# Phase carry through DRAM and GpSimd, phases kept in the arctangents' buffer, slot sums taken by the exponential

## The chip, the cores and the metric

The kernel runs on one core of one Trainium2 chip. The metric is the device time of one execution in microseconds (us). Three runs of the kernel before are shown, and one further execution was profiled; all durations, waits and gaps below come from that profiled execution.

## The reference

All is fp32. A gated linear attention (4 batches, 8 heads, 768 steps, head width 48) feeds a mixture of experts in which every expert owns 4 slots, and that feeds a two-layer network with a leaky ReLU:

```
scale = minimum(mag, 0.999) / (mag + 1e-06)          # mag = |a|
a_re_n, a_im_n = a_re * scale, a_im * scale
for t in range(768):
    new_re = ar * S_re - ai * S_im                   # the complex decay of step t
    new_im = ar * S_im + ai * S_re
    S_re, S_im = new_re + k[t] (x) v[t], new_im
    y[t] = q[t] . S_re
x = y as 3072 x 384
logits = x @ phi                                     # 32 slots
slot_input = softmax over tokens(logits).T @ x       # 32 x 384
slot_out[e] = relu(slot_input[e] @ w1[e]) @ w2[e]    # 8 experts, F = 1024
x = softmax over slots(logits) @ slot_out
out = leaky(x @ w_in) @ w_out                        # 384 -> 2048 -> 384
```

## The kernel before

**Units.** The attention is cut into 12 units: 6 chunks of 128 steps times 2 pairs of batches. Steps lie on the partitions, and a row of 768 columns holds 16 groups (2 batches x 8 heads) of width 48. Unit u and unit u+2 are the same sequences, one chunk later. The recurrence is done in chunks: with the logarithm of the decay's modulus and its phase summed over the steps of a chunk, q and k are multiplied by exp, cos and sin (`prep4`, L623 and L632), and attention in the chunk is a masked product (`mB` to `mC`, L662, L665, L688), to which the state `S` of the earlier chunks is added; `mD` (L703, L713 to L716) brings the state forward by the decay column `dc`.

**The phase of a unit.** `prep2` (L554) takes the arctangent in place in the buffer `im` on ScalarE. From the third unit on, GpSimd then starts a DMA that adds the carried phase to row 0 of `im` (L557). `phase` multiplies by a triangle of 1/2pi on TensorE (L570, `tri_p`), so that each row is the running sum in turns. ScalarE adds a large constant to round it (L581), VectorE subtracts it and the sum again (L582), which leaves minus the part of a turn in `cs[:, 1]`, and a bitwise AND puts its magnitude into `cs[:, 0]` (L583). `prep3` takes the two sines in place (L593, L594). For the unit two further on, VectorE multiplies rows 96 to 127 of `cs[:, 1]` by -2pi into a buffer `cr` of the tag `w` (L586), of which only row 127 is used.

**The decay of a unit.** `decay` (L606, L607) takes two exponentials of the running sum; its last row goes by SyncE's queue to a DRAM buffer `dr` and comes back as the columns `dc` (L611, L613). The same queue carries all loads, in order.

**Slots.** After each second unit `slots` forms the logits of 512 steps (L748), their running maximum, the exponential `e` with the maximum as bias (L756), and the products for `acc`; VectorE sums `e` along its rows (L778, in the first round L782) and updates the denominator `den` (L779).

**After the attention.** The expert weights come in 64 slabs of 384 KB into buffers as they become free (`load_slabs`; tag `w` has 33 buffers). `layer1` (L924) and `layer2` (L960) use them, then `product` and the two layers of the network (L1022, L1039 to L1041) follow.

**What sets the order.** The program is written as operations with costs, and a planner (`Plan.emit`, `backward`, `forward`) orders every engine's instructions by them: it repeats a backward and a forward pass and keeps the order with the earliest planned end. A different cost or a different operation can therefore move instructions on all engines. The table functions of ScalarE keep a fixed order among themselves (`turns`). Buffers are handed out by tags with a fixed number of buffers; a load waits on SyncE's queue until its buffer is free, and what is queued behind it waits too.

Of the kernel before, what the change touches and what calls it, by code (L numbers as in the profile page):

```python
# [24 lines left out]
P = 128  # L25
# [3 lines left out]
W = G * D  # L29
# [67 lines left out]
class Plan:  # L97
# [9 lines left out]
    def add(self, eng, cost, fn, r=(), w=(), table=None, nbytes=0, after=()):  # L107
        o = Op()
        if eng == "SP":
            cost = 0.06 + nbytes / 0.36e6  # L110
# [209 lines left out]
def tile_kernel(  # L320
# [69 lines left out]
    t_dr = Tag(dram, "dr", [W], 3)  # L390
# [93 lines left out]
    def cuts(u):  # L484
        return parts.get(u, [(0, W)])
# [64 lines left out]
    def prep2(u):  # L550

        im = st[u]["im"]
        for o, e in cuts(u):
            table(("A", u), "T", e - o, lambda x=slice(o, e): A.activation(im()[:, x], im()[:, x], AF.Arctan), [], [(im, o)])  # L554
        if u >= 2:
            cr = st[u - 2]["cr"]
            plan.add("POOL", 1.0, lambda: GP.dma_start(im()[0:1, :], cr()[127:128, :], accum_op=ALU.add), [cr], [(im, o) for o, _ in cuts(u)], nbytes=3072)  # L557
# [14 lines left out]
    def phase(u):  # L572
# [5 lines left out]
        for (ct, c0), (o, e) in zip(piles(u, (b_tr, b_tr, b_c)), cu):  # L578
            n, x, z = e - o, slice(o, e), slice(o - c0, e - c0)
            pe(n / 600 + 0.02, lambda ct=ct, c0=c0, o=o, e=e: sums(ct, c0, [(tri_p, im)], o, e), [(im, o)], [(ct, o)])  # L580
            act(n + 100, lambda x=x, z=z, ct=ct: A.activation(cs()[:, 1, x], ct()[:, z], AF.Identity, bias=b_rnd), [(ct, o)], [(cs, 1, o)])  # L581
            dve(c_dve(n), lambda x=x, z=z, ct=ct: V.scalar_tensor_tensor(cs()[:, 1, x], cs()[:, 1, x], RND, ct()[:, z], op0=ALU.subtract, op1=ALU.subtract), [(ct, o)], [(cs, 1, o)])  # L582
            dve(c_dve2(n), lambda x=x: V.tensor_scalar(cs()[:, 0, x].bitcast(I32), cs()[:, 1, x].bitcast(I32), 0x7FFFFFFF, None, op0=ALU.bitwise_and), [(cs, 1, o)], [(cs, 0, o)])  # L583
        if u + 2 < NU:
            cr = s["cr"] = t_w()
            dve(c_dve2(W), lambda: V.tensor_scalar(cr()[96:128], cs()[96:128, 1], -TWO_PI, None, op0=ALU.mult), [(cs, 1, o) for o, _ in cu], [cr])  # L586

    def prep3(u):

        cs = st[u]["cs"]  # L590
        for o, e in cuts(u):
            n, x = e - o, slice(o, e)
            table(("S", u), "T", n, lambda x=x: A.activation(cs()[:, 1, x], cs()[:, 1, x], AF.Sin, scale=-TWO_PI), [], [(cs, 1, o)])  # L593
# [144 lines left out]
    def slots(c):  # L738
# [17 lines left out]
        table(("L", c), "E", 128, lambda: A.activation(e(), b()[:, :P], AF.Exp, bias=n1), [b, ("nm", c + 1)], [e])  # L756
# [17 lines left out]
        sm = t_sm()  # L774
        sm1 = lambda: sm()[:, 0:1]
        if c:
            dve(c_dve(384), lambda: V.scalar_tensor_tensor(acc, acc, al(), b3()[:, :DM], op0=ALU.mult, op1=ALU.add), [b3, al], ["acc"])
            dve(0.2, lambda: V.tensor_reduce(sm1(), e(), axis=AX.X, op=ALU.add), [e], [sm])  # L778
            dve(0.1, lambda: V.scalar_tensor_tensor(den, den, al(), sm1(), op0=ALU.mult, op1=ALU.add), [sm, al], ["den"])  # L779
        else:  # L780
            dve(c_dve(384), lambda: V.tensor_copy(acc, b3()[:, :DM]), [b3], ["acc"])
            dve(0.2, lambda: V.tensor_reduce(den, e(), axis=AX.X, op=ALU.add), [e], ["den"])  # L782
# [361 lines left out]
```

## Time and profile before

| what | us |
|---|---|
| three runs, median (lowest to highest) | 513.94 (513.3 to 515.96) |
| the profiled execution, whole | 515.49 |
| its span in the trace | 513.6 |
| PE, DVE, ACT busy in the span | 480.4, 330.5, 357.5 |
| share of the last-ending chain: PE, DVE, ACT, DMA | 66%, 19%, 7%, 4% |

PE is TensorE's matrix products, DVE VectorE, ACT ScalarE, POOL GpSimd, SP SyncE. The span is 1.9 us shorter than the execution. Three stages are to be told apart by their windows: the attention from about 20 to 250 us, the experts from 252 to 284 us, and the two-layer network from 284 us to the end. The busy time of PE is modelled for pipelined matrix products, so where it reads full it has to be compared with how closely the products follow each other.

### The profile page before, as it was taken

To read this page: it belongs to the slowest core of one execution; us is meant where nothing else is said; L and a number is where in the kernel's file an instruction comes from. 1 tells how busy PE (TensorE), PEld (TensorE's weight loads), DVE (VectorE), ACT (ScalarE), POOL (GpSimd) and SP (SyncE) were. 2 spreads that over 40 slices of the span, in tenths; PEclk is the share of its full clock that TensorE was granted. 3 is DMA by queue.
4 is the path that set the end of the run, shared out by engine and by line. 5 is a ranking of instruction groups with operands and counts; after the bars stand their busy time and mean duration, and the time that the engine had idled before them with its cause. 6 is when DMAs were issued, how large, how long until landed. Compare 5 with 4: busy or idle time off the path is not lost.

```text
span 513.6 us, 10264 instructions
## 1 busy us (share of the span) xinstructions
PE 480.4 (94%) x3985; PEld 433.8 (84%) x3985; DVE 330.5 (64%) x705; ACT 357.5 (70%) x702; POOL 13.0 (3%) x27
## 2 busy tenths in 40 slices
PE   2597989999999999999799999999999999999997
PEld 1386868888889888889554899999999999999997
DVE  3597999999999998997533999514500552025300
ACT  6799999999989999864203899339900993069502
POOL 1000000000000000001000000000000000000000
PEclk9999999999999999999899999999999999999999
DMA  7955254364543757579799321000000110010102
GB/s 254 392 164 158 60 186 154 95 170 141 155 125 126 238 165 247 176 252 368 251 367 387 111 61 33 1 32 30 33 1 0 47 47 2 1 46 2 46 1 92
DMA packets 43844, 66.97 MB, mean 130 GB/s; under 512 B 19098, under 2 KB 24970, under 8 KB 43796
## 3 DMA queue, kind: packets, MB, share of 16 engines
q1 hardware_dynamic: 43476, 66.29, 38.9%
q8 instruction: 31, 0.51, 0.4%
q0 software_dynamic: 320, 0.03, 0.1%
q14 instruction: 17, 0.14, 0.1%
HBM read 61.53 MB, written 4.75 MB: 129 GB/s over the span
## 4 chain that ended last, share of the span: by engine, by line
PE 66%; DVE 19%; ACT 7%; DMA 4%; issue 2%; SPq 1%; POOL 0%; ACTq 0%; DVEq 0%; POOLq 0%
PE b L1039 13%; PE b L1040 13%; PE b L1041 13%; PE b L1022 4%; PE bsc L662 4%; PE bm L688 4%; PE btr L647 3%; PE b L924 2%; DVE sc L665 2%; PE bc L570 2%; DVE k L632 2%; PE bsc L703 2%; PE b L960 2%; DVE q L632 2%; DVE w L526 2%
## 5 line engine op out<-in xcount | busy, mean ns | idle before, releaser
L1026 DVE TENSOR_TENSOR w<-x,w 128x384 fp32r<-128x384 f32 x128 | 67.8, 554 | 106.0 <-ACT w L1025 105.9
L1039 PE MATMUL b<-w 128*128 128x384 f32 x384 | 128.6, 335 | 0.8 <-ACT x L1024 0.8
L1040 PE MATMUL b<-w 128*128 128x384 f32 x384 | 128.7, 335 | 0.0
L1041 PE MATMUL b<-w 128*128 128x384 f32 x384 | 128.3, 334 | 0.0
L1039 PEld LDWEIGHTS b<-w 128*128 128x128 f32 x384 | 72.1, 188 | 1.0 <-ACT x L1024 1.0
L1041 PEld LDWEIGHTS b<-w 128*128 128x128 f32 x384 | 72.1, 188 | 0.0
L1040 PEld LDWEIGHTS b<-w 128*128 128x128 f32 x384 | 72.1, 188 | 0.0
L1048 ACT ACTIVATE k<-b 128x384 f32<-128x384 f32 x24 | 11.3, 487 | 82.5 <-PE b L1041 82.3
L1025 ACT ACTIVATE w<-x 128x384 fp32r<-128x384 f32 x128 | 62.9, 531 | 6.1 <-PE b L1041 5.0
L1024 ACT ACTIVATE x<-b 128x384 f32<-128x384 f32 x128 | 58.7, 494 | 3.8 <-PE b L1022 3.1
L662 PE MATMUL bsc<-qt,kt 96*128 96x128 f32 x384 | 52.6, 283 | 1.8 <-DVE S L715 0.8
L662 PEld LDWEIGHTS bsc<-qt,kt 96*128 96x128 f32 x384 | 47.1, 194 | 5.4 <-issue 1.9
L688 PE MATMUL bm<-sc,w 128*64 128x128 f32 (+1 forms) x384 | 36.3, 277 | 0.1
L665 DVE TENSOR_TENSOR sc<-bsc,tri_r 128x512 f32<-128x512 f32 x48 | 32.6, 683 | 3.0 <-PE bsc L662 2.8
L186 ACT ACT_TABLE_LOAD x25 | 32.1, 1283 | 1.2 <-PEq L1133 0.8
L647 PE MATMUL btr<-ident,q 128*96 128x128 f32 x192 | 30.3, 281 | 1.9 <-ACT qt L653 1.0
L703 PEld LDWEIGHTS bsc<-w,k 128*96 128x96 f32 x320 | 29.0, 165 | 3.4 <-DVE sc L665 2.5
L703 PE MATMUL bsc<-w,k 128*96 128x48 f32 x320 | 30.3, 247 | 1.6 <-DVE sc L665 1.6
L688 PE MATMUL bm<-qt,S 96*48 96x128 f32 x320 | 31.1, 272 | 0.0
L647 PE MATMUL btr<-ident,k 128*96 128x128 f32 x192 | 29.9, 280 | 1.3 <-ACT w L525 0.7
L653 ACT ACTIVATE qt<-btr 96x512 f32<-96x512 f32 x48 | 28.2, 590 | 3.6 <-PE btr L647 3.5
L647 PEld LDWEIGHTS btr<-ident,q 128*96 128x96 f32 x192 | 21.5, 130 | 6.4 <-ACT qt L653 1.7
(173 smaller groups left out, 791.3 us busy)
## 6 DMA issues: line engine op xcount, KB each, us to landing
w<-in_w_dram SPq DMA_DIRECT2D x49, 384.0 KB, 6.3
w<-in_qkv_dram SPq DMA_DIRECT2D x36, 384.0 KB, 5.8
w<-in_a_dram SPq DMA_DIRECT2D x22, 384.0 KB, 4.6
w<-in_wi_dram SPq DMA_DIRECT2D x16, 384.0 KB, 4.3
w<-in_wo_dram SPq DMA_DIRECT2D x16, 384.0 KB, 5.4
out_dram<-k SPq DMA_DIRECT2D x24, 192.0 KB, 1.9
cs<-in_w_dram SPq DMA_DIRECT2D x6, 384.0 KB, 6.0
k<-in_w_dram SPq DMA_DIRECT2D x6, 192.0 KB, 6.1
```

What stands on the lines that cost most here:

```text
L186: self.preload(TABLES[name])
L647: T.transpose(b()[:96, P * i:P * i + P], src()[:, i].rearrange("p t d -> p (t d)"), ident)
L662: T.matmul(b()[:, P * i:P * i + P], lhsT=k()[:96, i, :], rhs=q()[:96, i, :], start=True, stop=True)
L665: dve(c_dve(512), lambda: V.tensor_tensor(t(), b().rearrange("p (i t) -> p i t", t=P), tri.unsqueeze(1).to_broadcast([P, 4, P]), op=ALU.mu ...
L688: T.matmul(y()[64 * j:64 * j + m, o:o + P], lhsT=l, rhs=r, start=kind == 0, stop=kind == 1 or c == 0)
L703: T.matmul(b()[:96, D * i:D * i + D], lhsT=ks[i // 4]()[:, i % 4].rearrange("p t d -> p (t d)"), rhs=v()[:, D * g:D * g + D], start=True, ...
L1024: act(NG, lambda: A.activation(u(), b()[:, :NG], AF.Prelu, alpha=0.01), [b], [u])
L1025: act(NG, lambda: A.activation(g()[:, 0], u(), AF.Copy), [u], [(g, 0)])
L1026: dve(c_dve(NG), lambda: V.tensor_tensor(g()[:, 1], u(), g()[:, 0].bitcast(F32), op=ALU.subtract), [u, (g, 0)], [(g, 1)])
L1039: T.matmul(b()[:, :DM], lhsT=lh, rhs=wh()[:, i], start=f == FO[0], stop=False)
L1040: T.matmul(b()[:, :DM], lhsT=ll, rhs=wh()[:, i], start=False, stop=False)
L1041: T.matmul(b()[:, :DM], lhsT=lh, rhs=wl()[:, i], start=False, stop=f == FO[-1])
```

## The change

- The rounded phase is written to `im` instead of `cs[:, 1]`: the two steps on it work in place in `im`, the AND and the first sine read `im` and write `cs`. So `im` is held until the sine, and `cs[:, 1]` is not written before it.
- The multiplication of 32 x 768 by -2pi on VectorE (10 instructions) goes. In its place, for each of the 10 units, SyncE's queue takes row 127 of `im` to DRAM, brings it back as a tile `cr` of 128 x 6, GpSimd multiplies that tile, and SyncE's queue takes it to DRAM again; the accumulating DMA of GpSimd reads it from there. That is 3 DMAs more on SyncE's queue and 1 instruction more on GpSimd for each.
- The exponential of the slots writes its row sums itself (`accum_out`), so VectorE's 6 sums go.
- The planner charges a DMA on SyncE's queue at least 0.45 us; the tag `dr` has 8 buffers instead of 3.

```diff
         if eng == "SP":
-            cost = 0.06 + nbytes / 0.36e6
+            cost = max(0.45, 0.06 + nbytes / 0.36e6)
...
-    t_dr = Tag(dram, "dr", [W], 3)
+    t_dr = Tag(dram, "dr", [W], 8)
+    t_cr = Tag(mem, "cr", [P, W // P], 2)
...
-            plan.add("POOL", 1.0, lambda: GP.dma_start(im()[0:1, :], cr()[127:128, :], accum_op=ALU.add), [cr], [(im, o) for o, _ in cuts(u)], nbytes=3072)
+            plan.add("POOL", 1.0, lambda: GP.dma_start(im()[0:1, :], cr().unsqueeze(0), accum_op=ALU.add), [cr], [(im, o) for o, _ in cuts(u)], nbytes=3072)
...
-            act(n + 100, lambda x=x, z=z, ct=ct: A.activation(cs()[:, 1, x], ct()[:, z], AF.Identity, bias=b_rnd), [(ct, o)], [(cs, 1, o)])
-            dve(c_dve(n), lambda x=x, z=z, ct=ct: V.scalar_tensor_tensor(cs()[:, 1, x], cs()[:, 1, x], RND, ct()[:, z], op0=ALU.subtract, op1=ALU.subtract), [(ct, o)], [(cs, 1, o)])
-            dve(c_dve2(n), lambda x=x: V.tensor_scalar(cs()[:, 0, x].bitcast(I32), cs()[:, 1, x].bitcast(I32), 0x7FFFFFFF, None, op0=ALU.bitwise_and), [(cs, 1, o)], [(cs, 0, o)])
+            act(n + 100, lambda x=x, z=z, ct=ct: A.activation(im()[:, x], ct()[:, z], AF.Identity, bias=b_rnd), [(ct, o)], [(im, o)])
+            dve(c_dve(n), lambda x=x, z=z, ct=ct: V.scalar_tensor_tensor(im()[:, x], im()[:, x], RND, ct()[:, z], op0=ALU.subtract, op1=ALU.subtract), [(ct, o)], [(im, o)])
+            dve(c_dve2(n), lambda x=x: V.tensor_scalar(cs()[:, 0, x].bitcast(I32), im()[:, x].bitcast(I32), 0x7FFFFFFF, None, op0=ALU.bitwise_and), [(im, o)], [(cs, 0, o)])
         if u + 2 < NU:
-            cr = s["cr"] = t_w()
-            dve(c_dve2(W), lambda: V.tensor_scalar(cr()[96:128], cs()[96:128, 1], -TWO_PI, None, op0=ALU.mult), [(cs, 1, o) for o, _ in cu], [cr])
+            row = t_dr()
+            cr = t_cr()
+            carried = s["cr"] = t_dr()
+            plan.add("SP", 0, lambda: SY.dma_start(row().unsqueeze(0), im()[P - 1:P, :]), [(im, o) for o, _ in cu], [row], nbytes=3072)
+            plan.add("SP", 0, lambda: SY.dma_start(cr(), row().rearrange("(p f) -> p f", p=P)), [row], [cr], nbytes=3072)
+            pool(0.12, lambda: GP.tensor_scalar(cr(), cr(), -TWO_PI, 0.0, op0=ALU.mult, op1=ALU.add), [], [cr])
+            plan.add("SP", 0, lambda: SY.dma_start(carried().rearrange("(p f) -> p f", p=P), cr()), [cr], [carried], nbytes=3072)
...
-            table(("S", u), "T", n, lambda x=x: A.activation(cs()[:, 1, x], cs()[:, 1, x], AF.Sin, scale=-TWO_PI), [], [(cs, 1, o)])
+            table(("S", u), "T", n, lambda x=x: A.activation(cs()[:, 1, x], im()[:, x], AF.Sin, scale=-TWO_PI), [(im, o)], [(cs, 1, o)])
...
-        table(("L", c), "E", 128, lambda: A.activation(e(), b()[:, :P], AF.Exp, bias=n1), [b, ("nm", c + 1)], [e])
+        sm = t_sm()
+        sm1 = lambda: sm()[:, 0:1]
+        table(("L", c), "E", 128, lambda: A.activation(e(), b()[:, :P], AF.Exp, bias=n1, accum_out=sm1() if c else den), [b, ("nm", c + 1)], [e, sm if c else "den"])
...
-            dve(0.2, lambda: V.tensor_reduce(sm1(), e(), axis=AX.X, op=ALU.add), [e], [sm])
...
-            dve(0.2, lambda: V.tensor_reduce(den, e(), axis=AX.X, op=ALU.add), [e], ["den"])
```

The planner gives another order on every engine. Three places are shown; the lines of the changed kernel are numbered one higher than those before from L353 to L586, and six higher from L606 to L755.

VectorE at the second unit, before: L582 and L583 are its phase (the L583 row is the last of it), L586 the multiplication for the carry, L517 the first step of the third unit (its ratio of imaginary to real part), L526, L543 and L546 that unit's moduli and logarithms, L665 the mask of the first unit's attention.

```order
L632 TENSOR_TENSOR q<-w,cs 128x384
L632 TENSOR_TENSOR k<-w,cs 128x384
L651 COPY kt<-btr 96x512
L665 TENSOR_TENSOR sc<-bsc,tri_r 128x512
L586 TENSOR_SCALAR w<-cs 32x768
L517 TENSOR_TENSOR w<-w 128x768
L665 TENSOR_TENSOR sc<-bsc,tri_r 128x512
L526 SCALAR_TENSOR_TENSOR w<-w 128x768
L543 TENSOR_SCALAR w<-w 128x768
L546 SCALAR_TENSOR_TENSOR w<-w 128x768
```

The same place of the changed kernel, VectorE (L583 and L584 are the phase of the second unit, L518 the ratio, L527, L544 and L547 the moduli and logarithms, L671 the mask):

```order
L638 TENSOR_TENSOR k<-w,cs 128x384
L583 SCALAR_TENSOR_TENSOR w<-w,bc 128x768
L584 TENSOR_SCALAR cs<-w 128x768
L518 TENSOR_TENSOR w<-w 128x768
L657 COPY kt<-btr 96x512
L527 SCALAR_TENSOR_TENSOR w<-w 128x768
L671 TENSOR_TENSOR sc<-bsc,tri_r 128x512
L544 TENSOR_SCALAR w<-w 128x768
L547 SCALAR_TENSOR_TENSOR w<-w 128x768
```

The first step of the third unit now stands ahead of the copy and of the first mask; before, it stood behind both and behind the multiplication.

VectorE at the third unit's phase, before (L446 to L448 are a conversion of the network's weights, `narrow`; L713 the first state of a pair of batches):

```order
L582 SCALAR_TENSOR_TENSOR cs<-cs,bc 128x768
L583 TENSOR_SCALAR cs<-cs 128x768
L665 TENSOR_TENSOR sc<-bsc,tri_r 128x512
L586 TENSOR_SCALAR w<-cs 32x768
L651 COPY kt<-btr 96x512
L713 TENSOR_TENSOR S<-bsc,dc 96x384
L446 TENSOR_SCALAR w<-w 128x384 x2
L447 TENSOR_SCALAR w<-w 128x384
L665 TENSOR_TENSOR sc<-bsc,tri_r 128x512
L447 TENSOR_SCALAR w<-w 128x384
L448 SCALAR_TENSOR_TENSOR w<-w 128x384 x2
```

The same place of the changed kernel (L719 is the first state, L629 and L638 are the next unit's q and k):

```order
L583 SCALAR_TENSOR_TENSOR w<-w,bc 128x768
L584 TENSOR_SCALAR cs<-w 128x768
L719 TENSOR_TENSOR S<-bsc,dc 96x384
L657 COPY kt<-btr 96x512
L671 TENSOR_TENSOR sc<-bsc,tri_r 128x512
L719 TENSOR_TENSOR S<-bsc,dc 96x384
L629 TENSOR_TENSOR w<-w 128x768
L671 TENSOR_TENSOR sc<-bsc,tri_r 128x512
L638 TENSOR_TENSOR q<-w,cs 128x384
```

The conversion's instructions are gone from this place; in the changed kernel the first of them stands behind the fifth unit's phase step.

SyncE's queue around the fifth unit's decay row, before (L493 loads `a`, L352 q, k, v or weights, L611 takes the decay row out, L613 brings it back):

```order
L352 DMA w<-in_wi_dram 128x768
L493 DMA w<-in_a_dram 128x768
L352 DMA w<-in_qkv_dram 128x768 x2
L493 DMA w<-in_a_dram 128x768
L611 DMA dr<-w 1x768
L352 DMA w<-in_qkv_dram 128x768
L613 DMA dc<-dr 48x16x1 x2
```

The same place of the changed kernel (L589, L590 and L592 are the three DMAs of the carry, L617 and L619 the decay row's):

```order
L589 DMA dr<-w 1x768
L590 DMA cr<-dr 128x6
L494 DMA w<-in_a_dram 128x768
L352 DMA w<-in_wi_dram 128x768
L592 DMA dr<-cr 128x6
L352 DMA w<-in_qkv_dram 128x768
L494 DMA w<-in_a_dram 128x768
L617 DMA dr<-w 1x768
L352 DMA w<-in_qkv_dram 128x768 x2
L619 DMA dc<-dr 48x16x1 x2
```

Ahead of the decay row there now stand the three DMAs of the carry, each of which needs the one before it (the last one GpSimd's product too), with two loads of `a`, one of weights and one of q, k, v between them.

## Rows read from the trace of the kernel before

**Rows 1.** Busy time of each engine by stretch (windows; the header names the columns).

```profile
core 0: us, PE busy (x) PEld busy (x) DVE busy (x) ACT busy (x) POOL busy (x), PEclk, DMA share, GB/s
...
20.00:40.00 20.00, 17.91 (x122) 14.99 (x122) 15.39 (x28) 16.93 (x27) 0.92 (x1) 1.00 0.63 213
...
60.00:80.00 20.00, 17.98 (x185) 14.08 (x184) 19.95 (x37) 19.71 (x33) 0.76 (x1) 1.00 0.62 185
...
260.00:280.00 20.00, 19.28 (x252) 9.09 (x248) 5.82 (x34) 3.68 (x7) 0.70 (x2) 1.00 1.03 402
```

**Rows 2.** VectorE's phase steps of the fifth, seventh and twelfth unit (timeline: start, us).

```profile
84.51 0.94 DVE L582 SCALAR_TENSOR_TENSOR cs<-cs,bc 128x768 f32<-128x768 f32 x1
...
119.44 0.95 DVE L582 SCALAR_TENSOR_TENSOR cs<-cs,bc 128x768 f32<-128x768 f32 x1
...
210.40 0.94 DVE L582 SCALAR_TENSOR_TENSOR cs<-cs,bc 128x768 f32<-128x768 f32 x1
```

**Rows 3.** TensorE's products packed closest (chain of waits: start, us, what, instructions).

```profile
185.32 1.01 PE bm L748 x32
...
189.21 1.29 PE bc L570 x4
190.61 0.89 PE bsc L662 x8
...
195.20 0.39 PE bm L728 x4
195.59 1.07 PE bc L570 x6
...
198.13 1.32 PE bsc L703 x16
199.45 0.88 PE btr L647 x8
200.33 1.90 PE bm L688 x31
```

**Rows 4.** What goes (one line each: ns min/median/max), and who waited for L586.

```profile
L586 DVE TENSOR_SCALAR w<-cs x10: 556/557/558, 21.8 to 178.2; 32x768 f32<-32x768 f32 x10
...
  ACT cs L593: 1.2, 1
...
L778 DVE TENSOR_REDUCE sm<-dd x5: 271/275/279, 124.7 to 248.4; 128x1 f32<-128x128 f32 x5
```

**Rows 5.** The chain of waits at the second unit (start, us, what).

```profile
31.64 0.56 DVE w L586
32.23 0.96 DVE w L517
```

**Rows 6.** An instruction of a conversion on VectorE (groups by line, 84 to 210 us).

```profile
L448 DVE SCALAR_TENSOR_TENSOR w<-w 128x384 int32<-128x384 int32 x10 | 5.2, 547 | 0.0
```

**Rows 7.** ScalarE's exponential of the slots, and its one-column exponential (one line each).

```profile
L756 ACT ACTIVATE dd<-bsc,nm x1: 367/367/367, 247.7 to 247.7; 128x128 f32<-128x128 f32 x1
...
L759 ACT ACTIVATE sm<-mx,nm x5: 283/293/294, 111.7 to 248.2; 128x1 f32<-128x1 f32 x5
```

**Rows 8.** GpSimd: the ninth unit's carry DMA (timeline), time to landing, its only tensor_scalar.

```profile
138.01 0.76 POOL L557 DMA_DIRECT2D w<-w  x1 [16.38 <-ACT w L554]
...
DMA to landing us min/median/max: 1.8/3.0/5.3
...
L868 POOL TENSOR_SCALAR kt<-logits x8: 351/352/527, 235.7 to 268.9; 128x192 fp32r<-128x192 f32 x8
```

**Rows 9.** SyncE's queue: loads, decay row; VectorE: their users (timeline).

```profile
113.51 7.91 SPq L352 DMA_DIRECT2D w<-in_qkv_dram  x3
...
126.36 0.25 SPq L611 DMA_DIRECT2D dr<-w  x1
...
142.83 0.96 DVE L623 TENSOR_TENSOR w<-w 128x768 f32<-128x768 f32 x1 [0.32 <-ACT w L606]
...
161.82 0.54 DVE L716 TENSOR_TENSOR S<-S,dc 96x384 f32<-96x384 f32 x1
```

More of the change, by code (lines that the diff above doesn't have):

```diff
@@ L588, in prep3 @@
     def prep3(u):
-        cs = st[u]["cs"]
+        cs, im = st[u]["cs"], st[u]["im"]
         for o, e in cuts(u):
             n, x = e - o, slice(o, e)
-            table(("S", u), "T", n, lambda x=x: A.activation(cs()[:, 1, x], cs()[:, 1, x], AF.Sin, scale=-TWO_PI), [], [(cs, 1, o)])
+            table(("S", u), "T", n, lambda x=x: A.activation(cs()[:, 1, x], im()[:, x], AF.Sin, scale=-TWO_PI), [(im, o)], [(cs, 1, o)])
             table(("S", u), "T", n, lambda x=x: A.activation(cs()[:, 0, x], cs()[:, 0, x], AF.Sin, bias=b_hpi, scale=-TWO_PI), [], [(cs, 0, o)])
@@ L773, in slots @@
         pe(0.9, ms, [dd] + [k for x in xs for k in ((x, 0), (x, 1))], [b3])
-        sm = t_sm()
-        sm1 = lambda: sm()[:, 0:1]
         if c:
             dve(c_dve(384), lambda: V.scalar_tensor_tensor(acc, acc, al(), b3()[:, :DM], op0=ALU.mult, op1=ALU.add), [b3, al], ["acc"])
-            dve(0.2, lambda: V.tensor_reduce(sm1(), e(), axis=AX.X, op=ALU.add), [e], [sm])
             dve(0.1, lambda: V.scalar_tensor_tensor(den, den, al(), sm1(), op0=ALU.mult, op1=ALU.add), [sm, al], ["den"])
```

## The prediction

> **What bounds the kernel now.** I read the windows first, then the instructions of VectorE and TensorE in order of time, then the chain of waits, then the queues. The change touches only the attention, so only the stretch up to about 240 us is argued over. In the windows [rows 1] the reader should see two things: VectorE is full from 60 us on (19.95 of 20 us) while TensorE still has holes (17.98 of 20), and from 20 to 40 us neither is full, which is the latency of the first units. After that TensorE's busy time reads full too, but it is modelled, so I compare it with the closest packing that the chain shows [rows 3]. One unit needs 4 x 0.88 for its transposes (L647), 4 x 0.89 for the scores (L662), 2 x 1.90 for the values and the state's part (L688), 2 x 1.32 for the new state (L703), 2 x 0.39 for the outputs' transposes (L728), 1.29 and 1.07 for the two running sums (L570), and half of 1.01 for the logits (L748): 3.52 + 3.56 + 3.80 + 2.64 + 0.78 + 2.36 + 0.50 = 17.2 us, without the slots' few other products. The phase steps of the fifth and the twelfth unit start 125.89 us apart [rows 2], seven units, so 17.98 us each. So between 84 and 210 us TensorE leaves at most 0.8 us a unit, 5.6 us in all, however much work VectorE loses; before 84 us VectorE and latency decide.
>
> **VectorE's multiplication (L586).** Ten instructions go, 556 ns each [rows 4]; on the engine one takes a step of 0.59 us, since its successor starts 32.23 - 31.64 later [rows 5]. That is 5.9 us in all. Three of them, at 31.6, 54.2 and 67.8 us (the ten lie between 21.8 and 178.2 [rows 4]), stand where VectorE decides, and the first of these is itself on the chain of waits [rows 5]: 3 x 0.59 = 1.8 us, all of it gained. The earliest one, at 21.8 us, made the first sine wait 1.2 us [rows 4], since that sine overwrites what L586 read; now it doesn't. The engine behind it has other work, so between 0 and 1.2 us, taken as 0.6. The other six, at 86 to 178 us, are 3.5 us in the stretch where TensorE is nearly full.
>
> **VectorE's sums (L778).** Six go, 275 ns each [rows 4], 1.6 us; all but one of them fall behind 84 us, the last at 248.4 us, where VectorE waits for others anyway. I put four, 1.1 us, with the six multiplications: 4.6 us of VectorE in a stretch that can give at most 5.6 us. Bounds 0 (TensorE takes all of it) and 4.6; I take 1.0, since 17.2 leaves out the slots' small products, I don't expect a perfect packing, and the next part brings work into this stretch.
>
> **What is moved.** In the orders shown, the third unit's first steps stand ahead of a copy and a mask, and the conversion of weights leaves the third unit: before, eight of its instructions on VectorE (none over 547 ns [rows 6]) stood ahead of the fifth unit's phase step, and now none does; ahead of the last unit's stand 48 in both. So up to 8 x 0.55 = 4.4 us of VectorE goes out of the stretch where VectorE decides, into one where TensorE does, and is paid back there as far as VectorE still decides. Bounds 0 and 4.4; I take 1.5.
>
> **ScalarE's exponential with sums.** No row shows it. The nearest are the same exponential without sums, 367 ns, and a whole one-column exponential, 283 to 294 ns [rows 7]. So it costs between 0 and 0.29 us, six times, at most 1.7 us; a gain is excluded, since ScalarE does all that it did and more. One, the last, lies on a serial stretch at 248 us; I take 0.1 us for that and 0.1 for the other five together.
>
> **The carry's new way.** SyncE's queue takes three DMAs more a unit: at the decay row's 0.25 us [rows 9] to about 0.5 each, some 1 us of issue in 18, beside other work. In latency: the carry's DMA on GpSimd lands after 3.0 us in the median [rows 8]; with that for each of the three, 0.25 + 3.0 + 0.5 + 3.0 + 0.5 + 3.0 us of DMA and 0.36 us for GpSimd's product (the row with 192 columns [rows 8]; here there are 6), 10.6 us. The seventh unit's phase step ends at 120.4 us [rows 2], and its carry is added for the ninth unit at 138.01 us, held up by the arctangent and not by the carry [rows 8]: 17.6 us. So 7 us are left for waiting on SyncE's queue, and that hides it. If that cover went, GpSimd would add the carry later, and TensorE's sum would wait.
>
> What the new DMAs delay on SyncE's queue is covered too. The eighth unit's q, k and v are issued by 121.4 us and first used at 142.83 us; the seventh unit's decay row leaves at 126.36 us and its columns are first multiplied in at 161.82 us [rows 9]. A delay of 10 us in either costs nothing. A buffer of the tag w is no longer held from one phase to the next unit's arctangent, and im is held until the sine instead: loads start no later for it. On GpSimd's queue the product stands behind the earlier unit's accumulating DMA, which waits for an arctangent; that is what the third rival is about.
>
> **GpSimd beside VectorE.** Ten small products now run while VectorE is full. Every tensor_scalar of GpSimd that the trace holds lies at 235.7 us or later [rows 8], so no row shows the two in the busy stretch. Bounds: 0 and 10 x 0.36 = 3.6 us of VectorE, if VectorE stood still for each; I take 0.3, as 6 columns are far from 192. The Trainium skill (SBUF — State Buffer, "Who interferes with whom") speaks against this edit: a GpSimd instruction that reads SBUF holds a port pair that VectorE's instructions with two SBUF inputs need, and whichever comes second stands still for the whole instruction. No run here shows it yet; by that rule the cost would be nearer 3.6 us and the sum nearer 1 us of gain, by the rows it is open between the two ends.
>
> **Behind the attention.** From about 252 to 284 us the experts wait for the attention's last sums and then for slabs that need buffers which they free themselves; from 260 to 280 us the DMA engines are full (1.03, 402 GB/s [rows 1]). An earlier end of the attention moves that stretch as a whole. I cost it at nothing, and plus or minus 1 us for the new order of loads.
>
> **The sum.** 1.8 + 0.6 + 1.0 + 1.5 = 4.9 us gained, 0.2 + 0.3 = 0.5 us paid: 4.4 us. Against the profiled execution's own 515.49 us (span 513.6 and 1.9 around it) that is 511.1 us. This execution is 1.55 us above the median of the runs, so the median should go from 513.94 to **509.5 us**. The parts' bounds are 1.8 + 0 + 0 + 0 less 1.7 and 3.6, a loss of 3.5, and 1.8 + 1.2 + 4.6 + 4.4 = 12.0 us of gain; not all ends come together.
>
> **Rivals.**
> 1. *TensorE already decides, and the early gain is eaten by the new order.* For it: 17.2 of 17.98 us a unit, and ScalarE at 19.71 of 20 from 60 us [rows 1], which loses nothing. Against it: VectorE is full and loses 7 us. Then only 1.8 us remain, less 0.5: 512.6 us, no change that can be measured. Chance 0.22.
> 2. *GpSimd stops VectorE.* As a mechanism of this kernel: each of the ten products holds VectorE up for 0.36 us, 3.6 us of the 4.9: 513.94 - 4.9 + 3.6 + 0.2 = 512.8 us. For it: VectorE is full when they run. Against it: 6 columns, not 192. Chance 0.06. (It is what the page of the Trainium skill named above, SBUF — State Buffer, would make of this change.)
> 3. *SyncE's queue and GpSimd's queue wait for each other.* In each unit the last carry DMA waits on SyncE's queue for GpSimd's product, which stands behind the accumulating DMA, which waits for an arctangent on ScalarE. If that arctangent comes late, loads stand still; once they stand for more than the 15 us or so by which q and k are early (142.83 less 121.4 and some 6 for the landing [rows 9]), VectorE's first product of the unit waits, and TensorE with it. It would come in every unit from the fourth on; 1 us in each of nine is 9 us, 513.94 - 4.4 + 9 = 518.5 us, slower. Against it: GpSimd's wait ended by the arctangent within 1 us of it [rows 8], and the queue had 7 to 20 us of cover. Chance 0.12.
> 4. *VectorE's freed time counts in full, as the new order packs TensorE better.* 1.8 + 1.2 + 4.6, 2 of the 4.4, less 0.5 is 9.1 us: 504.8 us. Chance 0.10.
>
> **How the numbers follow.** My forecast, 507 to 511.4 us, has 0.50. Faster by over 0.5% (2.6 us, below 511.4, about what a measurement of this kernel can tell from no change) is it and rival 4: 0.60. Within 0.5% are rivals 1 and 2: 0.28. Slower by over 0.5% is rival 3: 0.12. The range leaves out rival 3 and the far end of rival 4, and takes in the bounds of GpSimd's and ScalarE's cost: 505.0 to 515.5 us.
>
> **What the profile of the changed kernel would show.** If I am right: the twelfth unit's phase step starts 4 to 5 us earlier, with some 3 to 4 us of that already at the fifth unit's; between these two the spacing falls from 17.98 to about 17.8 us; the stretch from the last mask of the attention to the network's first product keeps its length; the accumulating DMAs still wait for arctangents. GpSimd's product below 0.2 us and VectorE's durations unchanged would settle rival 2. Rival 1 shows as an unchanged spacing and an unchanged start of the fifth unit's phase step, rival 3 as VectorE or TensorE waiting for a DMA or GpSimd. I am wrong above all if the new order loses in the first units what L586 gives, or if the stretch behind the attention grows because slabs come later.

## The result

The kernel got slower. Its median is 518.93 us (517.85 to 520.17, 6 runs) against 515.46 us for the kernel before in the same runs, a ratio of 1.0086, with a 95% interval of 1.0066 to 1.0107. The forecast was 509.5 us and the range ended at 515.5. The profiled execution takes 519.2 us, with a span of 517.5 against 513.6 us.

The windows of the changed kernel (the columns are those of [rows 1]):

```profile
20.00:40.00 20.00, 16.02 (x103) 13.38 (x104) 13.24 (x22) 17.10 (x26) 1.45 (x3) 0.91 0.71 204
60.00:80.00 20.00, 18.93 (x182) 15.04 (x183) 18.58 (x35) 19.81 (x33) 1.28 (x2) 1.00 0.56 141
100.00:120.00 20.00, 19.98 (x212) 17.46 (x213) 18.50 (x39) 18.14 (x34) 3.06 (x2) 0.91 0.44 122
240.00:260.00 20.00, 17.21 (x193) 11.36 (x195) 8.86 (x33) 6.08 (x21) 1.36 (x4) 0.74 0.69 246
260.00:280.00 20.00, 19.98 (x264) 9.35 (x253) 4.36 (x23) 2.47 (x5) 0.70 (x2) 1.00 1.02 392
280.00:300.00 20.00, 17.01 (x129) 14.33 (x129) 19.88 (x57) 15.17 (x38) 0.00 (x0) 1.00 0.41 131
```

The change did to VectorE what it says: from 60 to 80 us its busy time falls from 19.95 to 18.58 us, TensorE's rises from 17.98 to 18.93 [rows 1]. What is new stands in the third column from the end: the granted clock is 0.91 at 20 to 40 and at 100 to 120 us, where the kernel before had 1.00 in both, and 0.74 at 240 to 260 us, where it had 0.91. And at 280 to 300 us TensorE is busy for 17.01 us instead of 18.60. The kernel before in these windows:

```profile
240.00:260.00 20.00, 17.18 (x219) 12.23 (x221) 9.63 (x36) 6.34 (x19) 1.91 (x5) 0.91 0.79 284
280.00:300.00 20.00, 18.60 (x139) 16.26 (x129) 19.79 (x51) 16.37 (x40) 0.00 (x0) 1.00 0.34 113
...
100.00:120.00 20.00, 18.99 (x214) 16.05 (x212) 19.92 (x40) 19.02 (x31) 1.11 (x1) 1.00 0.59 180
```

**Where the 3.9 us of span come from.** Three points split the span: the slots' last exponential, the network's first product, and the end. The rows of before are its exponential at 247.75 us (L756) and its first product, here with TensorE's serial part between them (timeline: start, us):

```profile
248.17 0.33 PE L762 MATMUL bsc<-ident,dd 128*128 128x128 f32 x1 [1.39 <-ACT dd L756]
248.60 0.46 PE L893 MATMUL bsc<-kt,ones 128*128 128x128 f32 x2
...
249.16 0.85 PE L771 MATMUL bm<-x,dd 128*32 128x384 f32 x8
250.94 0.85 PE L903 MATMUL bm<-kt,acc 128*128 128x32 f32 x6 [0.93 <-DVE acc L777]
252.19 7.07 PE L924 MATMUL b<-w,dd 128*32 128x256 f32 x96 [0.40 <-issue]
...
284.23 0.69 PE L1022 MATMUL b<-q,qt 128*128 128x384 f32 x3
```

The same of the changed kernel, ScalarE's exponential first:

```profile
246.95 0.37 ACT L764 ACTIVATE dd<-bsc,nm 128x128 f32<-128x128 f32 x1 [1.26 <-DVE nm L761]
247.21 0.19 ACT L764 ACTIVATION_READ_ACCUMULATOR dd<-bsc,nm 128x1 f32 x1
...
247.46 0.33 PE L770 MATMUL bsc<-ident,dd 128*128 128x128 f32 x1 [1.49 <-ACT dd L764]
247.88 0.76 PE L897 MATMUL bsc<-kt,ones 128*128 128x128 f32 x2
...
248.78 1.51 PE L779 MATMUL bm<-x,dd 128*32 128x384 f32 x8
251.10 1.49 PE L907 MATMUL bm<-kt,acc 128*128 128x32 f32 x6 [0.81 <-DVE acc L783]
252.99 7.90 PE L928 MATMUL b<-w,dd 128*32 128x256 f32 x96 [0.40 <-issue]
...
285.85 0.68 PE L1026 MATMUL b<-q,qt 128*128 128x384 f32 x3
```

Up to the exponential 0.8 us are gained (247.75 to 246.95), and that is no merit of the change (what lies under this even part, fill_after shows below): TensorE's first product starts at 8.99 instead of 9.88 us here, and that differs from execution to execution (8.53 us in fill_before and 8.43 us in sums_only below, whose starts are those of the kernel before). From the exponential to the network's first product it takes 38.90 instead of 36.48 us, and the four groups of products shown account for all of that: 0.30 + 0.66 + 0.64 + 0.83 = 2.43 us. They have the same shapes; the first three run at half the clock, the fourth does so for longer than before:

```profile
248.00:250.00 2.00, 2.00 (x11) 0.65 (x11) 1.07 (x5) 0.96 (x4) 0.00 (x0) 0.50 0.17 59
...
256.00:258.00 2.00, 2.00 (x24) 1.10 (x20) 0.00 (x0) 0.00 (x0) 0.00 (x0) 0.50 0.63 181
```

In these windows the granted clock is 0.50, that is 1.2 GHz, from 248 to 258 us. In the kernel before it was 1.00 from 248 to 252 us and fell only in 252 to 256 us (0.64, then 0.51), when the short serial products were done:

```profile
252.00:254.00 2.00, 1.80 (x21) 1.19 (x25) 1.41 (x6) 0.36 (x1) 0.00 (x0) 0.64 0.53 167
254.00:256.00 2.00, 2.00 (x24) 1.31 (x20) 0.38 (x2) 0.00 (x0) 0.00 (x0) 0.51 0.22 46
```

The third part, from the network's first product to the end, takes 231.65 instead of 229.4 us. So -0.8 + 2.4 + 2.3 = 3.9 us. How the loss splits differs from execution to execution: no_floor below has the same order on TensorE, VectorE and ScalarE and the same span of 517.5 us, and its profiled execution loses 0.85 us in the second part and 3.8 us in the third, where its clock falls to 0.92 at 300 to 320 us.

**Why the third part grew.** TensorE's waits at the network's start in the changed kernel:

```profile
288.34 0.44 PE L1043 MATMUL b<-w 128*128 128x384 f32 x1 [0.75 <-ACT x L1028]
298.93 0.44 PE L1026 MATMUL b<-q,qt 128*128 128x384 f32 x1 [0.95 <-DVE qt L1014]
299.95 0.44 PE L1026 MATMUL b<-q,qt 128*128 128x384 f32 x1 [0.58 <-ACT x L1028]
300.98 0.44 PE L1026 MATMUL b<-q,qt 128*128 128x384 f32 x1 [0.58 <-ACT x L1028]
```

Before there was one such wait behind the first, of 0.58 us at 297.65 us. Now there are three, the first for a cast of VectorE (L1014) that stands behind the conversion of weights. Together they are 2.11 us instead of 0.58, which is 1.5 of the 2.3 us; where the rest arises was not followed. The chain of waits runs through that conversion:

```profile
296.78 0.55 DVE w L479
...
297.99 0.55 DVE w L450
298.54 0.34 DVE qt L1014
298.93 0.46 PE b L1026
```

Nothing was edited there. Counted from the first of VectorE's four casts in its order, the second, third and fourth stood 23, 28 and 46 instructions on; now they stand 23, 34 and 47, and the third is the one that TensorE waits for.

### The profile page after: what moved, and what is told of

Read it like the earlier page. It is cut to its first block, busy times and chain, and to the rows that moved or that the text cites. A ratio compares the mean times of both kernels' runs of the same rounds, so it can differ in the third digit from the quotient of the medians.

```text
span 517.5 us, 10327 instructions
## 1 busy us (share of the span) xinstructions
PE 485.1 (94%) x3985; PEld 436.5 (84%) x3985; DVE 324.5 (63%) x689; ACT 357.9 (69%) x708; POOL 20.0 (4%) x37
## 4 chain that ended last, share of the span: by engine, by line
PE 72%; DVE 12%; ACT 11%; issue 3%; DMA 1%; SPq 0%; POOL 0%; POOLq 0%; DVEq 0%; ACTq 0%
PE b L1045 12%; PE b L1043 12%; PE b L1044 12%; PE bm L694 5%; PE bsc L668 5%; PE btr L653 5%; PE b L1026 4%; PE bsc L709 3%; PE bc L571 3%; PE b L928 3%; ACT L186 2%; PE b L964 2%; DVE w L629 1%; DVE sc L671 1%; DVE q L638 1%
## 5 line engine op out<-in xcount | busy, mean ns | idle before, releaser
L694 PE MATMUL bm<-sc,w 128*64 128x128 f32 (+1 forms) x384 | 37.4, 283 | 0.2 <-DVE sc L671 0.2
L671 DVE TENSOR_TENSOR sc<-bsc,tri_r 128x512 f32<-128x512 f32 x48 | 32.8, 685 | 5.1 <-PE bsc L668 2.6
L1026 PE MATMUL b<-q,qt 128*128 128x384 f32 x80 | 25.1, 342 | 2.1 <-ACT x L1028 1.2
```

Of the source, the lines that this page charges most:

```text
L694: T.matmul(y()[64 * j:64 * j + m, o:o + P], lhsT=l, rhs=r, start=kind == 0, stop=kind == 1 or c == 0)
L1026: pe(0.17, lambda: T.matmul(b()[:, :NG], lhsT=w()[:, o:o + P], rhs=cT[j](), start=True, stop=True), [(w, o // 256), cT[j]], [b])
```

## The experiments

The ratios are to the kernel before in the same runs; the clock is the mean of the granted clocks of a kernel's runs (0.994 over 76 runs of the kernel before, 0.983 over the 6 of the changed one).

| kernel | median, us | ratio (95%) | clock |
|---|---|---|---|
| hold_order | 514.46 | 0.9996 (0.9983 to 1.001) | 0.993 |
| time_back | 522.54 | 1.0154 (1.0135 to 1.0173) | 0.981 |
| fill_after | 517.04 | 1.0047 (1.0032 to 1.0063) | 0.994 |
| fill_before | 514.44 | 1.0008 (0.999 to 1.0026) | 0.998 |
| no_floor | 518.75 | 1.008 (1.0049 to 1.0111) | 0.984 |
| carry_only | 515.98 | 1.0029 (1.0005 to 1.0053) | 0.989 |
| sums_only | 514.62 | 0.9995 (0.9974 to 1.0017) | 0.994 |
| after_light | 518.44 | 1.0063 (1.0038 to 1.0087) | 0.985 |
| cast_first | 516.14 | 1.0042 (1.002 to 1.0064) | 0.987 |
| fill_cast | 514.56 | 1.0009 (0.9992 to 1.0026) | 0.996 |
| hold_cast | 513.54 | 0.9983 (0.9971 to 0.9995) | 0.992 |
| other_order | 515.37 | 1.0019 (1.0003 to 1.0036) | 0.990 |

### hold_order: the new operations in the old order

The planner is given the operations of the kernel before; what they do when their turn comes is the change's. The multiplication's place holds only the first of the three DMAs, the other two and GpSimd's product go out behind a sine and an exponential.

```diff
+            def back():
+                SY.dma_start(cq(), row().rearrange("(p f) -> p f", p=P))
+                GP.tensor_scalar(cq(), cq(), -TWO_PI, 0.0, op0=ALU.mult, op1=ALU.add)
...
-            dve(c_dve2(W), lambda: V.tensor_scalar(cr()[96:128], cs()[96:128, 1], -TWO_PI, None, op0=ALU.mult), [(cs, 1, o) for o, _ in cu], [cr])
+            dve(c_dve2(W), carry, [(cs, 1, o) for o, _ in cu], [cr])
...
-            dve(0.2, lambda: V.tensor_reduce(sm1(), e(), axis=AX.X, op=ALU.add), [e], [sm])
+            dve(0.2, lambda: None, [e], [sm])
```

> All operations of the change (phases in the arctangents' buffer, the carry through DRAM and GpSimd, the sums by the exponential), but in the order that the kernel before has on TensorE, VectorE and ScalarE: the planner sees the old multiplication and the old sums, which are not made. Theory 1 (the operations themselves gain, the new order and the TensorE clock that falls in its gaps lose): ratio to before 0.991 to 0.998, 1 to 4.5 us faster. Rival (the new operations cost: queues, GpSimd): as slow as the changed kernel, ratio 1.005 to 1.01.

It comes out even, 0.9996, between the two ratios that I had expected. That says two things. The new operations cost nothing that can be measured, so the loss is the new order's. And in the time of the whole kernel they gain nothing either: VectorE is busy for 324.6 instead of 330.5 us, and these 5.9 us are worth at most 0.9 us (the interval's lower end) as long as the order stays. Whether a part of the kernel gained is left open: in the profiled execution, the fastest of its 10 runs, the last exponential comes 235.7 us after TensorE's first product, against 237.9 us before.

### time_back: VectorE's time put back into the new order

```diff
+            def mag(x=x):
+                if 0 < u < NU - 2:
+                    V.tensor_scalar(cs()[96:128, 0], im()[96:128], -TWO_PI, None, op0=ALU.mult)
```

> The changed kernel in its own order, with nine multiplications of 32 x 768 on VectorE put back (units 2 to 10; their result is overwritten), 9 x 0.59 = 5.3 us of VectorE. If VectorE's time counts on the path: 2 to 5 us over the changed kernel, 521 to 524 us. If TensorE and its clock decide: within 1 us of the changed kernel, 518 to 520 us.

It costs 3.6 us more than the changed kernel, for nine instructions that I put at 5.3 us (they take 557 ns each, 5.0 us). So in the new order VectorE's time does count, when it is added. In part it works through the clock: it is 0.83 at 60 to 80 us there.

```profile
60.00:80.00 20.00, 18.24 (x144) 14.54 (x142) 16.12 (x31) 17.14 (x28) 1.56 (x2) 0.83 0.55 140
```

### fill_after and fill_before: TensorE kept busy where it idles

Products that are needed anyway are issued again, at places ahead of which the clock fell: transposes in the first unit, scores in the fourth, and transposes beside the slots' last round and their softmax. The diff is fill_after's; fill_before repeats the transposes alone.

```diff
+MORE = {(0, 0, "k"): 3, (0, 1, "q"): 2}
...
-                for i in range(4):
+                for i in range(4 * more):
...
-            for i in range(4):
+            for i in [0, 1, 2, 3] * (2 if (u, hq) == (3, 3) else 1):
...
+            for i in range(7 if last else 0):
+                T.transpose(b2()[:, P:2 * P], lg(), ident)
...
-                for k in range(3):
+                for k in [0, 1, 2] * (1 + (4 if j == 5 else 0)):
```

> The changed kernel in its own order; TensorE repeats some products with the same inputs and outputs where it idled ahead of a fall of its granted clock: transposes at 25.4 and 28.2 us, one score group at 98.4 us, transposes at 246 and 250 us. Theory 1: the granted clock stays at its upper level at 100 to 104 and 248 to 258 us, and 2.5 to 5 us come back: 514 to 516.5 us. Rival (the clock is not what costs): 518.5 to 520 us.

> The kernel before in its own order with the same repeated transposes at 26.3, 246.6 and 250 us. Theory 1: the fall of the clock at 252 to 256 us goes away, 0.5 to 2 us faster, ratio 0.996 to 0.999. Rival (clock falls follow something else): ratio 1.000 to 1.002.

In the changed kernel the added work makes the kernel faster, by 1.9 us; its 517.04 us lie between the two ranges that I had expected. Windows of fill_after:

```profile
100.00:120.00 20.00, 20.00 (x222) 17.25 (x222) 19.93 (x41) 19.24 (x35) 1.28 (x3) 1.00 0.46 122
240.00:260.00 20.00, 17.63 (x249) 12.27 (x249) 8.82 (x38) 4.66 (x14) 0.68 (x2) 1.00 0.73 256
280.00:300.00 20.00, 17.13 (x88) 15.82 (x87) 19.47 (x49) 15.01 (x37) 0.00 (x0) 0.91 0.29 85
```

The clock is back at 1.00 at both places; from 20 to 40 us it is still 0.91. The network's start is as thin as in the changed kernel (17.13 us of TensorE), which is the other half, and the clock now falls there too, to 0.91.

What the fall at 100 us costs can be read from VectorE's phase steps on either side of it, in the changed kernel:

```profile
100.82 0.95 DVE L583 SCALAR_TENSOR_TENSOR w<-w,bc 128x768 f32<-128x768 f32 x1
...
120.43 0.95 DVE L583 SCALAR_TENSOR_TENSOR w<-w,bc 128x768 f32<-128x768 f32 x1
```

and in fill_after, which has the same order, with its last exponential:

```profile
99.88 0.95 DVE L584 SCALAR_TENSOR_TENSOR w<-w,bc 128x768 f32<-128x768 f32 x1
...
117.89 0.94 DVE L584 SCALAR_TENSOR_TENSOR w<-w,bc 128x768 f32<-128x768 f32 x1
...
244.40 0.37 ACT L765 ACTIVATE dd<-bsc,nm 128x128 f32<-128x128 f32 x1 [1.26 <-DVE nm L762]
```

The two steps are 19.61 us apart with the fall and 18.01 without it: 1.6 us. (They are 19.6 us apart in no_floor and cast_first, whose clock falls there too, and 18.0 in fill_cast, whose clock does not.) TensorE's first product starts at 8.99 us in both kernels, and fill_after's last exponential is 2.55 us earlier; the other 1 us of that arises in the first units, where the clock falls in both, and is not explained. So the even first part of the changed kernel hides two things: with the clock kept up at 100 us, the new order takes 235.4 us from the first product to the last exponential (fill_cast 235.4, too), 2.5 us less than the kernel before (237.9; fill_before 237.8), and the lower clock takes most of that back. These are single executions of each kernel.

In the kernel before, whose clock fell only behind the serial products, the addition brings nothing that can be measured, 1.0008, though the fall is gone from its profiled execution (mean clock 1.00); I had expected 0.1 to 0.4 percent.

### no_floor, carry_only, sums_only: which edit's order

no_floor takes only the planner's floor of 0.45 us for SyncE's DMAs back, which leaves the order on TensorE, VectorE and ScalarE as it is; carry_only takes back the floor and the sums; sums_only is the kernel before with the sums alone.

```diff
-            cost = max(0.45, 0.06 + nbytes / 0.36e6)
+            cost = 0.06 + nbytes / 0.36e6
```

> The changed kernel with only the planner's 0.45 us for a DMA of SyncE undone. TensorE, VectorE and ScalarE get the same instructions in the same order as in the changed kernel; only the order of SyncE's issues is other. If the changed kernel's loss lies in the order on the three engines (my theory now), this is as slow: 1.006 to 1.011 of the kernel before, 517.6 to 520.2 us, with the granted clock at the lower level near 100 us and near 250 us again. If it lies in when transfers start (rival: SyncE's new order), it comes back to 0.997 to 1.002, 513.0 to 515.6 us.

> The changed kernel without its new sums and without the 0.45 us: the six sums are VectorE's again, the phases and the carry go the new way, and the planner orders all of it anew. If the removal of the ten multiplications is what moves the phase steps ahead and opens the gaps on TensorE, it is slower than the kernel before by 0.4 to 1.1 percent, 516.5 to 520.1 us. Rival: the loss comes with the sums at the attention's end, then 0.997 to 1.002, 513.0 to 515.6 us. A gain over 0.4 percent would say that the operations gain in some orders and lose in others.

> The kernel before with only the sums brought by the exponential; six VectorE instructions of 275 ns are gone and the planner orders all anew. The work saved on the path is 0.3 us at most (the last sum lies where VectorE waits). If a new order alone can cost or gain more than the operations that it was made for, this one differs from the kernel before by more than 0.3 percent either way, 1.5 us; if the order is harmless, it lies within 0.2 percent, 513.5 to 515.6 us.

SyncE's order is not it: no_floor is as slow as the changed kernel, with the same clock. The sums alone give another order that costs nothing, the harmless one of the two cases that I had named; the carry alone costs 0.29 percent, between its two ranges. 0.29 and -0.05 do not add to 0.86: the loss belongs to no edit alone, it belongs to the order that the planner finds for both together.

### after_light and cast_first: the network's start

after_light leaves the maximum out of the conversion of the second weights; cast_first gives VectorE's four casts a lead of 3 us in the planner. Neither touches the attention.

```diff
-        dve(c_dve2(n), lambda: V.tensor_scalar(t1(), t1(), 2.0 ** -15, None, op0=ALU.max), [], [k1])
+        dve(c_dve2(n), lambda: None if light else V.tensor_scalar(t1(), t1(), 2.0 ** -15, None, op0=ALU.max), [], [k1])
```

```diff
                 if g % 2:
+                    plan.lead = 3.0
                     dve(c_dve(N), lambda g=g, y=y: V.tensor_copy(gs[g]()[:, y], b2[g]()[:, y]), [(b2[g], j)], [(gs[g], j)])
+                    plan.lead = 0.0
```

> The changed kernel without the maximum in the conversion of the network's second weights (one VectorE instruction of 0.35 us, 0.27 us in a row, for each of its chunks; the floor of the small magnitudes is left out of the computation). The changed kernel's network stage takes 231.7 us from its first product against 229.4 us before. If VectorE's conversion decides its start (theory), the stage gets 1.5 to 2.5 us shorter, TensorE's idle time at 290 to 302 us falls from 2.1 us to about the kernel before's 0.6 us, and the time is 516.4 to 517.6 us, 1.003 to 1.006 of the kernel before. If the stage is longer for another reason (slabs that land later, TensorE's own order), it stays within 0.3 us of 231.7 us and at 1.0086.

> The changed kernel with the four casts of the experts' product on VectorE (L1014 there) given 3 us of lead in the planner: the attention keeps its order on every engine, and in the network's start those casts go ahead of the weights' conversion. In the changed kernel TensorE waits 0.95, 0.58 and 0.58 us at 298.9 to 301.0 us for one such cast and for two round trips through ScalarE; in the kernel before once, 0.58 us. If the order of the network's start is what makes its stage 231.7 instead of 229.4 us (theory), the stage gets 1.0 to 2.3 us shorter and the time is 516.5 to 518 us, 1.003 to 1.006 of the kernel before. Rival: the stage is longer because VectorE has too much to convert in any order; then within 0.4 us of the changed kernel, 1.008.

Less work on VectorE hardly helps: the wait for the cast goes from 0.95 to 0.67 us, and the two of 0.58 us behind it, round trips through ScalarE that TensorE's own order makes, stay. The wait for the cast in after_light:

```profile
296.65 0.44 PE L1026 MATMUL b<-q,qt 128*128 128x384 f32 x1 [0.67 <-DVE qt L1014]
```

The first theory, too much to convert, is weak by that. It is not settled: the stage was not shorter in the profiled execution (232.9 us), but the clock was lower there (0.98 at 280 to 300 and 0.93 at 300 to 320 us), and the ratio, 1.0063, lies just above the range of the theory with an interval that overlaps the changed kernel's. Another order of the same work does help: cast_first's stage takes 230.5 instead of 231.65 us, and the wait for the cast is gone. TensorE's waits there:

```profile
287.61 0.44 PE L1045 MATMUL b<-w 128*128 128x384 f32 x1 [0.76 <-ACT x L1030]
298.00 0.45 PE L1028 MATMUL b<-q,qt 128*128 128x384 f32 x1 [0.58 <-ACT x L1030]
299.03 0.44 PE L1028 MATMUL b<-q,qt 128*128 128x384 f32 x1 [0.58 <-ACT x L1030]
```

The median fell by more than the stage, by 2.3 us when the ratios are compared; the runs of cast_first also had a somewhat higher clock (0.987 against 0.983), so a part of this gain may be the clock's.

### fill_cast: both at once

It is fill_after with the lead of cast_first; both diffs stand above.

> Both at once: the repeated TensorE products that keep its clock up in the attention (fill_after, which came to 1.0047) and the casts' lead at the network's start. If the loss is made of these two parts, clock and network start, and of nothing else, it comes back to the kernel before or just below: 512.5 to 515.5 us, 0.996 to 1.002. If one of the two is a side effect of the other, or something else is lost in the attention, it stays at 1.003 to 1.006.

1.0009: the loss is gone. Against the changed kernel the parts give 0.39 and 0.44 percent, together 0.83; measured are 0.77. So the loss is made of these two, the clock in the attention and its tail, and the order at the network's start, and the rest is within the intervals. How much belongs to each is less sure, since cast_first's clock rose as well.

### hold_cast and other_order: are orders good or bad by chance?

hold_cast is hold_order with the same lead of 3 us, other_order the changed kernel with a lead of 10 us for the same four casts, which makes the planner end with another of its rounds.

```diff
-                    plan.lead = 3.0
+                    plan.lead = 10.0
```

> All operations of the change in the order of the kernel before (hold_order, 0.9996), with the casts' lead at the network's start. There TensorE waits once for 0.58 us behind the first products, so 0.3 to 1.2 us are to be had if the lead helps: 512.5 to 514.3 us, 0.996 to 0.999. If the network's order was already good, 1.000 within 0.002; the lead can also make it worse, if conversion then comes late: up to 1.004.

> The changed kernel with 10 us of lead for the same four casts, which lie behind the attention: it makes the planner choose another of its rounds, so the attention too gets another order of the same instructions. If the order, not the work, sets the time within some 1 percent (theory), it differs from the changed kernel by more than 1 us either way, anywhere from 512 to 521 us, and its mean granted clock goes along: above 0.990 it is below 516.5 us, below 0.985 above 517 us. If the work that was moved sets the time, it is at 1.007 to 1.010 again, whatever its clock.

other_order has the changed kernel's instructions and is 3.5 us faster, by a number that concerns four casts behind the attention. It also shows what VectorE's phase step is worth as a sign. Its twelfth unit's (VectorE) and the serial products (TensorE):

```profile
214.66 0.94 DVE L583 SCALAR_TENSOR_TENSOR w<-w,bc 128x768 f32<-128x768 f32 x1
...
250.64 0.85 PE L779 MATMUL bm<-x,dd 128*32 128x384 f32 x8
252.43 0.85 PE L907 MATMUL bm<-kt,acc 128*128 128x32 f32 x6 [0.93 <-DVE acc L783]
253.68 7.07 PE L928 MATMUL b<-w,dd 128*32 128x256 f32 x96 [0.40 <-issue]
```

The step comes 4.3 us later than in the kernel before [rows 2] and 7.0 us later than in the changed one; L928 starts only 0.7 us after the changed kernel's, and then takes 7.07 instead of 7.90 us, as in the kernel before: the clock falls there from 254 to 258 us alone (0.51, then 0.63). hold_cast is the only kernel whose interval lies below the kernel before; its 0.17 percent are less than the half percent that I called measurable.

## Why the prediction was wrong

**What bounds the kernel.** VectorE full from 60 us on with TensorE close behind was read rightly, and the change turned the two around there. But the bound was used for the wrong question. A full engine says that work added to it costs (time_back, 3.6 us for 5.3 us); it doesn't say that work taken away gains (hold_order, 0.9996).

**The terms of the gain, 1.8 + 0.6 + 1.0 + 1.5 us.** This is the first step that failed. The signs that I had named were there in part: the twelfth unit's phase step

```profile
207.65 0.94 DVE L583 SCALAR_TENSOR_TENSOR w<-w,bc 128x768 f32<-128x768 f32 x1
```

is 2.75 us earlier than in [rows 2] (4 to 5 were forecast), the fifth unit's, at 82.28 us, 2.2 us (3 to 4 were forecast), of which 0.9 us each is the earlier first product; the spacing fell to 125.37 / 7 = 17.91 us, near the 17.8 forecast. But the last exponential was not earlier by more than those 0.9 us. Two things stand between. The sum took an earlier step for an earlier end: counted from the first product, the twelfth step is 1.9 us earlier than before and the exponential 0.1 us later; in fill_after they are 4.4 and 2.5 us earlier. (That phase steps run ahead of TensorE's work as far as buffers let them is my reading and not shown.) And it had no term for the clock in the attention: the fall at 100 us alone costs 1.6 us. Without that fall about half of the forecast gain was there, 2.5 of 4.4 us, by single executions. "All of it gained", said of the three early multiplications, was an assertion from one place on the chain of waits [rows 5]; one place on a chain says nothing of what is late next.

**Behind the attention, "I cost it at nothing".** This is the second step that failed, and the larger: 2.4 us to the network's first product and 2.3 us behind it (0.85 and 3.8 us in no_floor). "An earlier end moves that stretch as a whole" took for granted that products keep their durations and the network's start its order. The first depends on TensorE's clock, which the prediction never read although the windows' column stood in [rows 1]; the second on a planner that orders the whole program anew for every edit. The prediction did say that it would be wrong above all if this stretch grew "because slabs come later": it grew, but no slab was late. TensorE's weight loads wait for DMAs for 0.6 us in all in both kernels, and from 260 to 280 us the DMA engines are as full as before (1.02 against 1.03).

**Rivals.** Rival 1 (the gain is eaten, 512.6 us) named the right direction and stopped at zero. Rival 3 reached the right time, 518.5 us, by a mechanism that is not there, which is luck: VectorE waits for DMAs for 3.0 us in all, 2.4 before, TensorE for 0.6 us in both, and no_floor changes SyncE's order and not the time. GpSimd's accumulating DMA still waits for arctangents, in eight of ten cases, 90.8 us in all; the carry was covered, as forecast.

**GpSimd beside VectorE (rival 2, 0.3 us in the sum).** GpSimd's product, in the idlest and in the longest case (timeline), and in one line (ns min/median/max):

```profile
107.91 2.26 POOL L591 TENSOR_SCALAR cr<-cr 128x6 f32<-128x6 f32 x1 [6.60 <-DMA cr<-dr]
...
143.40 0.19 POOL L591 TENSOR_SCALAR cr<-cr 128x6 f32<-128x6 f32 x1 [4.38 <-DMA cr<-dr]
```

```profile
L591 POOL TENSOR_SCALAR cr<-cr x10: 190/412/2260, 25.7 to 177.9; 128x6 f32<-128x6 f32 x10
```

The rival had it the wrong way around. VectorE's durations are unchanged (its masks take 685 ns, 683 before; its products of 768 columns with ScalarE's exponentials 953 and 950 in the mean), and GpSimd is the one that stands still: 0.19 us at 143.4 us, where VectorE idles, 2.26 us from 107.91 to 110.17, while VectorE runs instructions with two inputs from SBUF until 110.02 us. The Trainium skill (SBUF — State Buffer, "Who interferes with whom") says that the one that comes first keeps the shared ports for its whole instruction. The trace agrees in that one of the two stands still, but 2.26 us is longer than any single instruction of VectorE there (0.95 us): GpSimd's record covers several that followed each other. What I drew from it, 0.36 us of VectorE for each product, was wrong in who waits; I take it that a product of 0.19 us rarely comes first against a full VectorE.

**ScalarE's sums (0.2 us).** Rightly sized where it can be read: the exponential is as long as before, 367 ns, and is followed by an instruction of its own that reads the sum, 0.19 to 0.22 us, six times. The last of them (shown above at 247.21) is near the path: TensorE's next product starts 0.51 us after the start of the exponential, 0.42 before, so 0.1 us. What the other five cost was not followed.

**Chances.** That the new order loses what the operations gain was written down as what would make the prediction wrong, and given no share of the chance on the slow side beyond rival 3's 0.12.

## What to carry to other kernels

When an edit makes a planner order everything anew, cost the edit and the new order apart: run the new operations in the old order first (here 0.9996), and only then the new order (1.0086). A freed microsecond on a full engine is worth something only if the order then gives that place to the engine that ends last, and an earlier step on a side engine is no measure of that; read the last serial step. A stretch that comes out even can hide a gain and a loss: here the same order with and without the fall of the clock told them apart. And read the clock's column stage by stage: a serial product that took 0.85 us took 1.5 when the clock fell just ahead of it.

## What the runs showed of the hardware

**The clock of TensorE falls after short idle times in a busy stretch, and idle times alone don't tell where.** At 100 us, in the changed kernel:

```profile
100.02 1.85 PE L709 MATMUL bsc<-w,k 128*96 128x48 f32 x16 [1.41 <-DVE sc L671]
...
102.27 0.65 PE L694 MATMUL bm<-qt,S 96*48 96x128 f32 x4
...
104.69 0.39 PE L694 MATMUL bm<-qt,S 96*48 96x128 f32 x4
```

TensorE had waited 1.41 us for a mask; at 102.27 us four products take 0.65 us, at 104.69 us four of the same shape 0.39 us. In the tail it waited 1.49 us ahead of L770 and ran at 0.50 from 248 us on. But other_order waits 1.38 us at the same place, the kernel before 1.39, hold_order 1.48 and sums_only 1.49 us, and the three short groups behind keep their full speed there (0.46, 0.85 and at most 0.86 us); hold_cast waits 1.49 us as well, and there they take 0.46, 1.51 and 1.49 us. So the length of the wait doesn't decide it alone; what else does was not settled.

**Lower clock and longer time go together from run to run, too.** Among runs of one kernel, those with a mean granted clock lower by 0.01 are 3.2 us longer (a fit within the 14 kernels). By that the changed kernel's 0.011 less than the kernel before would be 3.6 us. I read that as too high, since the stalls ahead of which the clock falls cost time themselves, and the 1.9 us of fill_after, whose added products take time too, as too low. The one fall that can be read by itself, at 100 us, costs 1.6 us.
